# A one-core attention and two-MLP kernel: another conversion of float64 weights, reciprocals spread by transposes, and fewer blocks in plain form

## The chip, the core and the metric

The kernel runs on one core of a Trainium2 chip. A core has TensorE (PE in the profile; its weight loads are PEld), VectorE (DVE), ScalarE (ACT), GpSimd (POOL) and SyncE (SP), which take their instructions in written order, each from its own list, and wait for one another by semaphores; transfers run on DMA queues that SP and POOL feed. The metric is device time in microseconds (us) of one execution, as the median of several runs.

## The reference

The reference is an attention over 4 batches, 12 heads, 448 positions and 64 elements per head, and two MLPs behind it on the 1792 x 768 result:

```
q_n, k_n = rmsnorm(q, g_q), rmsnorm(k, g_k)
scores = q_n @ k_n.T / 8;  scores = scores - max(scores)
attn = exp(scores);  attn = attn / (sum(attn) + 1e-9)
x = (attn @ v), heads side by side             # 1792 x 768
x = (sigmoid(x @ w_gate) * (x @ w_val)) @ w_out    # 768 -> 1536 -> 768
x = relu(x @ w_in) ** 2 @ w_out2                   # 768 -> 2048 -> 768
```

The weights w_gate, w_val, w_out, w_in and w_out2 lie in HBM as float64. Everything else is float32.

## The kernel before, in words

**Sweeps.** The MLPs run batch by batch, in four sweeps (`sweep(s)`, L519) of 448 positions. Each sweep needs all the weights, cut into NB = 68 blocks of 128 x 768 numbers: 24 of w_gate and w_val by turns, 12 of w_out, 16 of w_in, 16 of w_out2. Between the products of sweep s stand the steps of the attention of batch s+1, one slot after another (`slots_of`, L638). Batch 0's attention has no sweep to stand in: it is the prologue (L781), whose steps are laid out by hand as a list of due times, sorted, and kept in that order (`pinned`). Elsewhere the tile scheduler orders each engine's list.

**A product in three passes.** PE multiplies in a fast form of float32 (fp32r) that keeps fewer bits of each factor. So a matrix is split into a high part, its cast to fp32r, and a low part, the remainder, and `mm3` (L510 to 512) adds three products: high by high, high by low, low by high. A block's weights are split by `w_split` (L155): ACT casts the high part (L164), DVE subtracts (L165), both into one of four buffers `wsp`. x is split by `x_hi` (ACT, L334) and `x_lo` (DVE, L337).

**Plain products.** In sweep 0 the first NPLAIN = 12 blocks of w_gate and w_val are multiplied in plain float32 (L539), from batch 0's unsplit x, `xplain`. For these blocks the conversion writes straight into the `wsp` buffer, and `w_split` only stores it.

**The conversion.** In sweep 0 each block goes through four steps, which `w_ahead` (L168) issues some blocks ahead of the product:

- `w_load` (L110, L116): SP issues the load of the float64 block, 768 KB, into one of three buffers `raw`. Seen as pairs of 32-bit words, `lo` and `hi`.
- `w_conv` (L123): ACT scales `hi`, read as a float, by 2^-112 (L137), which moves the exponent to float32's place and leaves three bits of room; DVE takes the sign bit out of `hi` (L140), shifts ACT's result left by three and puts the sign back (L144), and puts in the top three bits of `lo` (L146). The result is a float32 block in `wraw` (three buffers) or, for plain blocks, in `wsp`.
- `w_store` (L153): POOL issues the store of the float32 block to a DRAM copy, `w`, 384 KB.
- `w_split`, as above.

Sweeps 1 to 3 load the float32 copies (L116's other branch, w into wraw), without conversion. The prologue's plan has the loads of blocks 0 to 4 and the conversions of blocks 0 and 1; further ones come where `w_ahead` finds room when block 0's product is issued, which is ahead of the prologue's last steps in the scheduler's view.

**Attention of batches 0 and 1.** A pair of heads `hp` is one unit; there are six pairs a batch. Per pair: a transpose of q and k (`a_mm`, `a_copy`, L256 and its neighbours), scores of four chunks of 112 rows (`s_mm`, L262), their maximum on DVE (L268), exponentials with sums `su` on ACT (L280, two a chunk), transposes of the result p (`c_mm`, L295) and copies of these (`c_copy`, L304 on ACT and a DVE copy), then `pv_mm` (L307): the product with v (L313), and a spread of the reciprocals. For that spread, `s_rec` (L285) takes the reciprocals of `su`, 112 x 4 x 2 numbers (L288), and eight small float32 matmuls against the identity (L318) write each of them into the 64 rows of its head in PSUM, 128 x 448. ACT copies it (`x_rec`, L326) and DVE multiplies (`x_sum`). Batches 2 and 3 divide otherwise, and use none of this.

**Rings.** Three `raw`, three `wraw`, four `wsp`, and four temporaries `tmp` (L54) of 128 x 512 that attention (squares, `rs`) and the MLPs (gate, ReLU, outputs) share. PSUM: four accumulators `acc` and two `att`.

Of the kernel before, what the change touches and what calls it, by code (L numbers as in the profile page):

```python
# [8 lines left out]
F32 = mybir.dt.float32  # L9
F32R = mybir.dt.float32r  # L10
I32 = mybir.dt.int32
AF = mybir.ActivationFunctionType
ALU = mybir.AluOpType
# [4 lines left out]
def attention_moe_moe2_kernel(  # L18
# [14 lines left out]
    nc = tc.nc  # L33
    B, H, S, D = q.shape
# [3 lines left out]
    KD = DM // 128  # L38
    K1 = F1 // 128
    K2 = F2 // 128  # L40
    HP = H // 2
    QC = 4
    QR = S // QC
# [4 lines left out]
    scale = 1.0 / float(D) ** 0.5  # L48
# [5 lines left out]
    tmp_p = ctx.enter_context(tc.tile_pool(name="tmp", bufs=4))  # L54
# [8 lines left out]
    ident = const.tile([128, 128], F32, name="ident")  # L63
# [33 lines left out]
        for kb in range(K2 // 2):  # L97
            one_sweep.append(rows64(w_out2, 2 * kb, 2, hf * 384, 384))
    NB = len(one_sweep)
    NPLAIN = K1  # L100
    NALL = NB * B

    w32 = [dram_p.tile([128, 768], F32, tag=f"w{i}", name=f"w{i}") for i in range(NB)]
# [19 lines left out]
    def w_conv():  # L123
        i = pos["conv"]
        pos["conv"] += 1
        if i >= NB:
            return
        r = raw64.pop(i).rearrange("p (f t) -> p f t", t=2)
        lo, hi = r[:, :, 0], r[:, :, 1]
        if i < NPLAIN:  # L130
            sp = wsp_p.tile([128, 2, 768], F32R, tag="wsp", name="wsp")
            t = sp[:, 0].bitcast(F32)
            wsp[i] = sp
        else:
            t = wraw_p.tile([128, 768], F32, tag="wraw", name="wraw")
        ti = t.bitcast(I32)
        size = nc.scalar.activation(out=t, in_=hi.bitcast(F32), func=AF.Copy, scale=2.0 ** -112)  # L137
        if pinned[0]:
            tc.keep_in_program_order(size)
        sign = nc.vector.tensor_scalar(  # L140
            out=hi, in0=hi, scalar1=-(2 ** 31), scalar2=None, op0=ALU.bitwise_and)
        if pinned[0]:
            tc.keep_in_program_order(sign)
        nc.vector.scalar_tensor_tensor(  # L144
            out=ti, in0=ti, scalar=3, in1=hi, op0=ALU.logical_shift_left, op1=ALU.bitwise_or)
        nc.vector.scalar_tensor_tensor(  # L146
            out=ti, in0=lo, scalar=29, in1=ti, op0=ALU.logical_shift_right, op1=ALU.bitwise_or)
        wraw[i] = t

    def w_store():  # L150
# [4 lines left out]
    def w_split():  # L155
        i = pos["split"]
        pos["split"] += 1
        if pos["store"] <= i < NB:
            w_store()
        t = wraw.pop(i)  # L160
        if i < NPLAIN:
            return
        sp = wsp_p.tile([128, 2, 768], F32R, tag="wsp", name="wsp")
        nc.scalar.copy(out=sp[:, 0], in_=t)  # L164
        nc.vector.tensor_tensor(out=sp[:, 1], in0=t, in1=sp[:, 0].bitcast(F32), op=ALU.subtract)  # L165
        wsp[i] = sp

    def w_ahead(i):  # L168
        while True:
            if pos["split"] <= min(i + 3, pos["conv"] - 1):  # L170
                w_split()
            elif pos["conv"] <= min(i + (3 if pos["conv"] < NPLAIN + 2 else 4), pos["load"] - 1, pos["split"] + 2):
                w_conv()
# [111 lines left out]
    def s_rec(st):  # L285
        su = st["su"]
        nc.vector.tensor_scalar(out=su, in0=su, scalar1=1e-9, scalar2=None, op0=ALU.add)
        nc.vector.reciprocal(out=su, in_=su)  # L288

    def c_mm(st, c, lo, hi):  # L290

# [15 lines left out]
    def pv_mm(st, o, rt):  # L307


        v, pt = st["v"], st.pop("pt")  # L310
        for kc in range(NF + 1):
            for e in range(2):
                nc.tensor.matmul(  # L313
                    out=o[e * D:(e + 1) * D], lhsT=v[:, kc, e], rhs=pt[:, (NF + 1) * e + kc if kc < NF else NF],
                    start=(kc == 0), stop=(kc == NF))
        for c in range(QC):
            for e in range(2):
                nc.tensor.matmul(  # L318
                    out=rt[e * D:(e + 1) * D, c * QR:(c + 1) * QR],
                    lhsT=st["su"][:, c, e:e + 1].to_broadcast([QR, D]), rhs=ident[:QR, :QR],  # L320
                    start=True, stop=True)
        st["o"], st["rt"] = o, rt

    def x_rec(st):
# [9 lines left out]
    def x_hi(st):  # L334
        nc.scalar.copy(out=xtile[st["b"]][:, 0, st["hp"]], in_=st["o"])

    def x_lo(st):  # L337
        x, hp = xtile[st["b"]], st["hp"]
        nc.vector.tensor_tensor(out=x[:, 1, hp], in0=st.pop("o"), in1=x[:, 0, hp].bitcast(F32), op=ALU.subtract)
# [144 lines left out]
    xtile, xplain = {}, {}  # L484
# [34 lines left out]
    def sweep(s):  # L519
# [11 lines left out]
        for m in range(K1):  # L531
            for i in range(2):
                o = acc_tile()[:, :N]
                wb = block()
                for kk in range(KD):
                    if s == 0 and m == 0 and i == 0 and kk == KD - 1:
                        yield
                    if s == 0 and 2 * m + i < NPLAIN:
                        nc.tensor.matmul(  # L539
                            out=o, lhsT=wb[:, 0, kk].bitcast(F32), rhs=xplain[0][:, kk],  # L540
                            start=(kk == 0), stop=(kk == KD - 1))
                    else:
                        mm3(o, wb, kk, x[:, 0, kk], x[:, 1, kk], kk == 0, kk == KD - 1)
                if s == 0 and 2 <= 2 * m + i < 2 + KD:
                    st = {"b": 0, "hp": 2 * m + i - 2, "o": xplain[0][:, 2 * m + i - 2]}
                    x_hi(st)
                    x_lo(st)
                if i == 0:
                    t = tmp("t")
                    e = tmp("e")  # L550
                    nc.scalar.activation(out=e, in_=o, func=AF.Relu, scale=-1.0)
                    nc.scalar.activation(out=t, in_=o, func=AF.Abs)
                    nc.scalar.activation(out=e, in_=e, func=AF.Exp, scale=-1.0)
                    nc.scalar.activation(out=t, in_=t, func=AF.Tanh, scale=0.5)
                else:
                    nc.vector.tensor_tensor(out=e, in0=o, in1=e, op=ALU.mult)
                    nc.vector.scalar_tensor_tensor(out=e, in0=t, scalar=1.0, in1=e, op0=ALU.add, op1=ALU.mult)
                    nc.scalar.copy(out=ht[:, 0, m], in_=e)
                    low.tensor_tensor(out=ht[:, 1, m], in0=e, in1=ht[:, 0, m].bitcast(F32), op=ALU.subtract)
                yield  # L560
        y = xbuf(s)
        for j2 in range(KD // 2):
            for i in range(2):
                o = acc_tile()[:, :N]
                for b2 in range(2):
# [4 lines left out]
                    if b2 == 1:  # L570
# [3 lines left out]
                            out=y[:, 1, j], in0=o, scalar=0.5, in1=y[:, 0, j].bitcast(F32),  # L574
                            op0=ALU.mult, op1=ALU.subtract)
# [7 lines left out]
        for m2 in range(K2 // 2):  # L583
            for i in range(2):
                m = 2 * m2 + i
                o = acc_tile()[:, :N]
# [3 lines left out]
                t = tmp("rl")  # L590
# [5 lines left out]
                for dst, d0, c0, cn in parts:  # L596
                    low.tensor_tensor(
                        out=dst[:, 1, m, d0:d0 + cn], in0=r2[:, c0:c0 + cn],
                        in1=dst[:, 0, m, d0:d0 + cn].bitcast(F32), op=ALU.subtract)
# [5 lines left out]
        for hf in range(2):  # L605
            accs = [acc_tile() for _ in range(nt)]
            for kb in range(K2 // 2):
                wb = block()
                for c, (rr, c0, row) in enumerate(chunks):
                    o = accs[c][:, :384]  # L610
# [283 lines left out]
    for r in range(2):  # L894
# [3 lines left out]
        out=gqk, in0=gains[:, 0:1], scalar=scale, in1=gains[:, 1:2], op0=ALU.mult, op1=ALU.mult)  # L898
# [49 lines left out]
```

## Time and profile before

| | |
|---|---|
| time, median of 3 runs | 1309.39 us (1307.68 to 1309.93) |
| the profiled execution | 1309.2 us, its span 1307.1 us |
| PE | 1284.9 us busy, 98% of the span, mean granted clock 0.997 |
| DVE | 938.4 us, 72% |
| ACT | 781.7 us, 60% |
| POOL | 130.3 us, 10% |
| DMA | 189.62 MB |

The span is the time from the first instruction to the last; the execution's own time has 2.1 us around it. The engines run side by side, so that shares do not add up. A share is an average over parts that differ: the prologue (to about 98 us), sweep 0 with its conversions (to about 430 us), and the three sweeps behind it.

### The profile page before, as it was taken

To read this page: it belongs to the slowest core of one execution; us is meant where nothing else is said; L and a number is where in the kernel's file an instruction comes from. 1 tells how busy PE (TensorE), PEld (TensorE's weight loads), DVE (VectorE), ACT (ScalarE), POOL (GpSimd) and SP (SyncE) were. 2 spreads that over 40 slices of the span, in tenths; PEclk is the share of its full clock that TensorE was granted. 3 is DMA by queue.
4 is the path that set the end of the run, shared out by engine and by line. 5 is a ranking of instruction groups with operands and counts; after the bars stand their busy time and mean duration, and the time that the engine had idled before them with its cause. 6 is when DMAs were issued, how large, how long until landed. Compare 5 with 4: busy or idle time off the path is not lost.

```text
span 1307.1 us, 19338 instructions
## 1 busy us (share of the span) xinstructions
PE 1284.9 (98%) x6899; PEld 1120.1 (86%) x6899; DVE 938.4 (72%) x1643; ACT 781.7 (60%) x1600; POOL 130.3 (10%) x100
## 2 busy tenths in 40 slices
PE   8999999999899999999999999999999999999998
PEld 6554488788697999999999999999999999999998
DVE  6876999899898678768986478877897544435521
ACT  5764687568666678656664477765676455524421
POOL 3201214210221001000010000100010000000000
PEclk9999999999899999999999999999999999999999
DMA  5426897787788434333343533434324343333331
GB/s 144 103 76 216 273 292 246 252 270 218 245 232 273 130 113 121 105 114 107 107 113 105 146 97 110 125 100 114 99 86 121 116 127 109 109 109 109 108 114 46
DMA packets 155807, 189.62 MB, mean 145 GB/s; under 512 B 76096, under 2 KB 119616, under 8 KB 155712
## 3 DMA queue, kind: packets, MB, share of 16 engines
q1 hardware_dynamic: 148416, 161.19, 43.0%
q0 software_dynamic: 5440, 26.74, 5.0%
q8 instruction: 55, 0.90, 0.3%
q10 hardware_dynamic: 1856, 0.46, 0.2%
q14 instruction: 40, 0.33, 0.1%
HBM read 150.60 MB, written 32.24 MB: 140 GB/s over the span
## 4 chain that ended last, share of the span: by engine, by line
PE 73%; issue 10%; DVE 7%; DMA 4%; ACT 4%; POOL 2%; POOLq 0%; ACTq 0%; SPq 0%; DVEq 0%
PE acc L510 15%; PE acc L511 15%; PE acc L512 15%; PE acc L617 5%; PE acc L615 5%; PE acc L616 5%; PE att L398 3%; PE att L439 2%; DMA w<-wraw 2%; PE att L470 2%; POOL ms L232 1%; DVE nm L268 1%; PE att L472 1%; ACT p L280 1%; PE acc L313 1%
## 5 line engine op out<-in xcount | busy, mean ns | idle before, releaser
L165 DVE TENSOR_TENSOR wsp<-wraw,wsp 128x768 fp32r<-128x768 f32 x260 | 248.0, 954 | 130.8 <-ACT wsp L164 125.9
L510 PE MATMUL acc<-xy,wsp 128*128 128x448 f32 x888 | 326.7, 368 | 0.2 <-ACT rl L592 0.2
L512 PE MATMUL acc<-xy,wsp 128*128 128x448 f32 x888 | 326.1, 368 | 0.0
L511 PE MATMUL acc<-xy,wsp 128*128 128x448 f32 x888 | 325.9, 367 | 0.0
L164 ACT CAST wsp<-wraw 128x768 fp32r<-128x768 f32 x260 | 216.6, 834 | 130.9 <-PE acc L617 64.7
L512 PEld LDWEIGHTS acc<-xy,wsp 128*128 128x128 f32 x888 | 166.9, 188 | 16.1 <-issue 2.7
L510 PEld LDWEIGHTS acc<-xy,wsp 128*128 128x128 f32 x888 | 166.8, 188 | 16.1 <-issue 0.9
L511 PEld LDWEIGHTS acc<-xy,wsp 128*128 128x128 f32 x888 | 166.9, 188 | 15.0 <-issue 1.5
L232 POOL TENSOR_TENSOR ms<-ms,mhalf 112x16 f32<-112x16 f32 (+1 forms) x25 | 91.1, 3648 | 577.1 <-DVE ms L231 486.8
L616 PE MATMUL acc<-wsp,rb 128*128 128x384 f32 x384 | 129.2, 336 | 0.0
L617 PE MATMUL acc<-wsp,rb 128*128 128x384 f32 x384 | 129.0, 336 | 0.0
L615 PE MATMUL acc<-wsp,rb 128*128 128x384 f32 x384 | 128.8, 335 | 0.0
L510 PE MATMUL acc<-hb,wsp 128*128 128x448 f32 x288 | 106.2, 369 | 0.0
L511 PE MATMUL acc<-hb,wsp 128*128 128x448 f32 x288 | 105.5, 367 | 0.0
L512 PE MATMUL acc<-hb,wsp 128*128 128x448 f32 x288 | 105.5, 367 | 0.0
L417 ACT ACTIVATE p<-att,nm,ms 112x448 f32<-112x448 f32 x96 | 68.8, 724 | 34.7 <-DVE nm L408 34.5
L137 ACT ACTIVATE wraw<-raw 128x768 f32<-128x768 f32 x56 | 51.5, 920 | 51.8 <-DMA w<-wraw 27.8
L592 ACT ACTIVATE rl<-acc 128x448 f32<-128x448 f32 x64 | 35.0, 547 | 70.7 <-PE acc L512 69.9
L280 ACT ACTIVATE p<-att,nm 112x448 f32<-112x448 f32 x88 | 55.3, 639 | 33.7 <-DVE nm L268 32.3
L617 PEld LDWEIGHTS acc<-wsp,rb 128*128 128x128 f32 x384 | 72.1, 188 | 1.6 <-issue 1.3
L616 PEld LDWEIGHTS acc<-wsp,rb 128*128 128x128 f32 x384 | 72.1, 188 | 0.8 <-issue 0.7
L615 PEld LDWEIGHTS acc<-wsp,rb 128*128 128x128 f32 x384 | 72.1, 188 | 0.2
(136 smaller groups left out, 2167.7 us busy)
## 6 DMA issues: line engine op xcount, KB each, us to landing
wraw<-w SPq DMA_DIRECT2D x204, 384.0 KB, 3.0
w<-wraw POOLq DMA_DIRECT2D x56, 384.0 KB, 6.0
raw<-in_moe_w_out_dram SPq DMA_DIRECT2D x28, 768.0 KB, 5.4
raw<-in_moe_w_in_dram SPq DMA_DIRECT2D x16, 768.0 KB, 6.6
raw<-in_moe_w_gate_dram SPq DMA_DIRECT2D x12, 768.0 KB, 6.8
raw<-in_moe_w_val_dram SPq DMA_DIRECT2D x12, 768.0 KB, 6.1
out_dram<-ob SPq DMA_DIRECT2D x28, 192.0 KB, 2.9
qs<-qs SPq DMA_DIRECT2D x24, 224.0 KB, 3.0
```

Of the source, the lines that this page charges most:

```text
L137: size = nc.scalar.activation(out=t, in_=hi.bitcast(F32), func=AF.Copy, scale=2.0 ** -112)
L164: nc.scalar.copy(out=sp[:, 0], in_=t)
L165: nc.vector.tensor_tensor(out=sp[:, 1], in0=t, in1=sp[:, 0].bitcast(F32), op=ALU.subtract)
L232: nc.gpsimd.tensor_tensor(out=ms, in0=ms, in1=mhalf[:QR, 0:ms.shape[1]], op=ALU.pow)
L280: nc.scalar.activation(out=p[:, e], in_=ps[:QR, e, :S], func=AF.Exp, bias=nm[:, e:e + 1], scale=st["rq"][:, c, e:e + 1] if "rq" in st else ...
L417: nc.scalar.activation(out=p[:, i * (S + TAIL):i * (S + TAIL) + S], in_=ps[:QR, i, :S], func=AF.Exp, bias=nm[:, i:i + 1], scale=rq[:, 2 * ...
L510: nc.tensor.matmul(out=o, lhsT=wh, rhs=xh, start=start, stop=False)
L511: nc.tensor.matmul(out=o, lhsT=wh, rhs=xl, start=False, stop=False)
L512: nc.tensor.matmul(out=o, lhsT=wl, rhs=xh, start=False, stop=stop)
L615: nc.tensor.matmul(out=o, lhsT=rh, rhs=wh, start=(k1 == 0), stop=False)
L616: nc.tensor.matmul(out=o, lhsT=rh, rhs=wl, start=False, stop=False)
L617: nc.tensor.matmul(out=o, lhsT=rl, rhs=wh, start=False, stop=(k1 == K2 - 1))
```

## The change

1. **NPLAIN** goes from 12 to 4: blocks 4 to 11 of sweep 0 are converted into `wraw`, split and multiplied in three passes.
2. **The conversion** has one DVE step less. ACT's function becomes a leaky one (`Prelu`, scale 2^-112, alpha 2^32): a negative number comes out 2^32 times larger, by which a bit stands where the shift by three leaves it as the sign. DVE's first step shifts `lo` right by 29 (into `hi`), its second shifts ACT's result and puts these three bits in. The third step goes.
3. **Reciprocals**: `s_rec` also lets POOL write `su` 64 times over into a temporary `sb` of 112 x 512, and `pv_mm` takes four transposes of it instead of eight matmuls. This holds for the twelve pairs of batches 0 and 1.
4. **x's split** for batch 0 moves from blocks 2 to 7 (one pair each) to blocks 0 to 2 (two pairs each), since block 4 needs it now.

```
-    NPLAIN = K1
+    NPLAIN = 4
...
-        size = nc.scalar.activation(out=t, in_=hi.bitcast(F32), func=AF.Copy, scale=2.0 ** -112)
+        size = nc.scalar.activation(
+            out=t, in_=hi.bitcast(F32), func=AF.Prelu, scale=2.0 ** -112, alpha=2.0 ** 32)
...
-        sign = nc.vector.tensor_scalar(
-            out=hi, in0=hi, scalar1=-(2 ** 31), scalar2=None, op0=ALU.bitwise_and)
+        low3 = nc.vector.tensor_scalar(
+            out=hi, in0=lo, scalar1=29, scalar2=None, op0=ALU.logical_shift_right)
...
         nc.vector.scalar_tensor_tensor(
             out=ti, in0=ti, scalar=3, in1=hi, op0=ALU.logical_shift_left, op1=ALU.bitwise_or)
-        nc.vector.scalar_tensor_tensor(
-            out=ti, in0=lo, scalar=29, in1=ti, op0=ALU.logical_shift_right, op1=ALU.bitwise_or)
...
         nc.vector.reciprocal(out=su, in_=su)
+        sb = st["sb"] = tmp_p.tile([128, 512], F32, tag="tmp", name="sb")[:QR].rearrange(
+            "p (c e d) -> p c e d", c=QC, e=2)
+        nc.gpsimd.tensor_copy(out=sb, in_=su.unsqueeze(3).to_broadcast([QR, QC, 2, D]))
...
+        sb = st.pop("sb")
         for c in range(QC):
-            for e in range(2):
-                nc.tensor.matmul(
-                    out=rt[e * D:(e + 1) * D, c * QR:(c + 1) * QR],
-                    lhsT=st["su"][:, c, e:e + 1].to_broadcast([QR, D]), rhs=ident[:QR, :QR],
-                    start=True, stop=True)
+            nc.tensor.transpose(
+                rt[:, c * QR:(c + 1) * QR], sb[:, c].rearrange("p e d -> p (e d)"), ident[:QR, :QR])
...
-                if s == 0 and 2 <= 2 * m + i < 2 + KD:
-                    st = {"b": 0, "hp": 2 * m + i - 2, "o": xplain[0][:, 2 * m + i - 2]}
-                    x_hi(st)
-                    x_lo(st)
+                if s == 0 and 2 * m + i < KD // 2:
+                    for hp in range(2 * (2 * m + i), 2 * (2 * m + i) + 2):
+                        st = {"b": 0, "hp": hp, "o": xplain[0][:, hp]}
+                        x_hi(st)
+                        x_lo(st)
```

The change also moves instructions on the engines' lists. From about 430 us on, all five lists stand as before. At the prologue's end, ACT's list holds the conversions of the blocks ahead (L137, told apart by the number of their `raw` buffer), the exponentials of the last two pairs (L280, after the change L279) and the copies of their transposes (L304, after the change L306). This is the stretch around the fifth pair's last chunks, before:

```order
L137 ACTIVATE wsp<-raw_598 128x768
L256 ACTIVATE kq<-acc,gqk 128x448
L280 ACTIVATE p,su<-att,nm 112x448 x2
L326 COPY rs<-acc 128x448
L304 COPY pt<-acc 128x4x112
L335 CAST xy_232<-xplain 128x448
L280 ACTIVATE p,su<-att,nm 112x448 x2
L304 COPY pt<-acc 128x4x112
L280 ACTIVATE p,su<-att,nm 112x448 x2
```

and after the change:

```order
L137 ACTIVATE wsp<-raw_596 128x768
L255 ACTIVATE kq<-acc,gqk 128x448
L279 ACTIVATE p,su<-att,nm 112x448 x2
L326 COPY rs<-acc 128x448
L306 COPY pt<-acc 128x4x112
L335 CAST xy_232<-xplain 128x448
L137 ACTIVATE wraw<-raw_915 128x768
L279 ACTIVATE p,su<-att,nm 112x448 x2
L306 COPY pt<-acc 128x4x112 x2
L279 ACTIVATE p,su<-att,nm 112x448 x2
```

Here raw_598 and raw_596 are block 1, raw_915 is block 4: its conversion now stands ahead of two exponentials. A little further on the same list, at the last pair, before:

```order
L280 ACTIVATE p,su<-att,nm 112x448 x4
L326 COPY rs<-acc 128x448
L304 COPY area<-acc 128x4x112
L335 CAST xy_232<-xplain 128x448
L280 ACTIVATE p,su<-att,nm 112x448 x2
L137 ACTIVATE wsp<-raw_710 128x768
L137 ACTIVATE wsp<-raw_826 128x768
L304 COPY area<-acc 128x4x112 x2
```

and after:

```order
L137 ACTIVATE wraw<-raw_1067 128x768
L279 ACTIVATE p,su<-att,nm 112x448 x2
L326 COPY rs<-acc 128x448
L306 COPY area<-acc 128x4x112
L279 ACTIVATE p,su<-att,nm 112x448 x2
L137 ACTIVATE wsp<-raw_706 128x768
L137 ACTIVATE wsp<-raw_819 128x768
L335 CAST xy_232<-xplain 128x448
L137 ACTIVATE wraw<-raw_1069 128x768
L306 COPY area<-acc 128x4x112 x2
```

Blocks 2 and 3 (raw_710 and raw_826, now raw_706 and raw_819) keep their place; the conversions of blocks 5 and 6 (raw_1067 and raw_1069) are new here, block 6's ahead of the last two copies. On POOL, which issues the stores (w with a number is a block's DRAM copy, 97 that of block 0), the same stretch reads before:

```order
L232 TENSOR_TENSOR ms<-ms,mhalf 112x16 x5
L153 DMA w_97<-wsp 128x768
L153 DMA w_98<-wsp 128x768
L153 DMA w_99<-wsp 128x768
L153 DMA w_100<-wsp 128x768
L232 TENSOR_TENSOR ms<-ms,mhalf 112x16
L153 DMA w_101<-wsp 128x768
```

and after:

```order
L231 TENSOR_TENSOR ms<-ms,mhalf 112x16
L152 DMA w_97<-wsp 128x768
L290 COPY sb<-su 112x512
L152 DMA w_98<-wsp 128x768
L152 DMA w_101<-wraw 128x768
L290 COPY sb<-su 112x512
L152 DMA w_102<-wraw 128x768
L290 COPY sb<-su 112x512
L152 DMA w_99<-wsp 128x768
L152 DMA w_100<-wsp 128x768
L152 DMA w_103<-wraw 128x768
```

The stores of blocks 4 and 5 (w_101, w_102) now stand ahead of those of blocks 2 and 3, and the copies of `su` between them.

## Rows read from the trace of the kernel before

**Rows 1.** Windows: length, busy PE, PEld, DVE, ACT, POOL; PE clock, DMA share, GB/s.

```profile
98.00:430.00 332.00, 320.37 (x1640) 248.04 (x1639) 290.54 (x429) 218.55 (x428) 68.39 (x71) 0.99 0.80 251
430.00:1307.00 877.00, 873.83 (x4668) 817.92 (x4667) 576.92 (x1087) 500.11 (x1018) 40.96 (x11) 1.00 0.37 109
```

**Rows 2.** Waits of PE from 98 us on: tile, releaser, us, times, longest.

```profile
PE att L313 <- ACT pt L304: 3.4, 1, 3.4
```

**Rows 3.** Timeline of PE: start, us, line; plain and three-pass products.

```profile
119.54 3.55 PE L539 MATMUL acc<-xplain,wsp 128*128 128x448 f32 x9
...
123.31 8.45 PE L539 MATMUL acc<-xplain,wsp 128*128 128x448 f32 x22
...
249.84 0.37 PE L512 MATMUL acc<-hb,wsp 128*128 128x448 f32 x1
...
252.88 0.37 PE L512 MATMUL acc<-hb,wsp 128*128 128x448 f32 x1
```

**Rows 4.** Timeline of PE in the prologue, the third pair's last product.

```profile
81.53 3.23 PE L313 MATMUL acc<-pt,v 128*64 128x448 f32 x16
84.59 0.94 PE L318 MATMUL acc<-ident,su 112*64 112x112 f32 x16
85.46 0.89 PE L295 MATMUL acc<-ident,p 112*128 112x112 f32 x7
86.28 1.01 PE L262 MATMUL att<-kq 64*112 64x448 f32 x4
```

**Rows 5.** Lines of DVE, 98 to 430 us: busy, mean ns | idle before, releasers.

```profile
L165 DVE TENSOR_TENSOR wsp<-wraw,wsp 128x768 fp32r<-128x768 f32 x58 | 55.1, 954 | 4.2 <-ACT wsp L164 3.5 <-DMA wraw<-w 0.6
...
L146 DVE SCALAR_TENSOR_TENSOR wraw<-raw,wraw 128x768 int32<-128x768 int32 x56 | 53.3, 952 | 0.2
...
L140 DVE TENSOR_SCALAR raw<-raw 128x768 int32<-128x768 int32 x64 | 35.8, 559 | 13.9 <-ACT wraw L137 10.4 <-ACT wsp L137 3.1
```

**Rows 6.** Lines of ACT, 98 to 430 us, columns as above.

```profile
L137 ACT ACTIVATE wraw<-raw 128x768 f32<-128x768 f32 x56 | 51.5, 920 | 51.8 <-DMA w<-wraw 27.8 <-DVE wsp L165 15.0 <-issue 2.5
...
L280 ACT ACTIVATE p<-att,nm 112x448 f32<-112x448 f32 x48 | 30.1, 635 | 23.8 <-DVE nm L268 23.8
```

**Rows 7.** Timeline of ACT and PE near 340 us, with idle; one window.

```profile
337.48 0.89 ACT L137 ACTIVATE wraw<-raw 128x768 f32<-128x768 f32 x1 [3.57 <-DMA w<-wraw]
...
341.60 6.19 PE L313 MATMUL att<-pt,v 128*64 128x448 f32 x16 [3.38 <-ACT pt L304]
...
340.00:348.00 8.00, 6.40 (x26) 4.28 (x28) 7.11 (x9) 3.64 (x6) 1.08 (x2) 0.57 0.63 178
```

**Rows 8.** Timeline of ACT, DVE and SP's queue in the prologue.

```profile
69.33 0.92 ACT L137 ACTIVATE wsp<-raw 128x768 f32<-128x768 f32 x1
...
76.91 0.63 ACT L280 ACTIVATE p<-att,nm 112x448 f32<-112x448 f32 x1 [1.75 <-DVE nm L268]
...
71.88 0.96 DVE L146 SCALAR_TENSOR_TENSOR wsp<-raw,wsp 128x768 int32<-128x768 int32 x1
...
73.39 0.54 SPq L116 DMA_DIRECT2D raw<-in_moe_w_gate_dram  x1
```

**Rows 9.** Timeline of one raw load and its reader; the queue's list.

```profile
112.92 0.37 SPq L116 DMA_DIRECT2D raw<-in_moe_w_val_dram  x1
...
118.08 0.91 ACT L137 ACTIVATE wsp<-raw 128x768 f32<-128x768 f32 x1 [4.30 <-DMA raw<-in_moe_w_val_dram]
...
raw<-in_moe_w_gate_dram SPq DMA_DIRECT2D x12, 768.0 KB, 6.8
```

**Rows 10.** Timeline of POOL: one operation early and one late.

```profile
222.16 7.65 POOL L232 TENSOR_TENSOR ms<-ms,mhalf 112x16 f32<-112x16 f32 x1 [0.72 <-DVE ms L231]
...
548.55 2.90 POOL L232 TENSOR_TENSOR ms<-ms,mhalf 112x16 f32<-112x16 f32 x1 [40.63 <-DVE ms L231]
```

**Rows 11.** Source views of two lines: ns min/median/max, first and last start.

```profile
L288 DVE RECIPROCAL su<-su x12: 191/196/203, 27.2 to 413.7; 112x8 f32<-112x8 f32 x12
...
L318 PE MATMUL att<-ident,su x96: 257/259/262, 193.7 to 425.3; 112*64 112x112 f32 x96
```

More of the change, by code (lines that the diff above doesn't have):

```diff
@@ L136, in w_conv @@
         ti = t.bitcast(I32)
-        size = nc.scalar.activation(out=t, in_=hi.bitcast(F32), func=AF.Copy, scale=2.0 ** -112)
+        size = nc.scalar.activation(
+            out=t, in_=hi.bitcast(F32), func=AF.Prelu, scale=2.0 ** -112, alpha=2.0 ** 32)
         if pinned[0]:
             tc.keep_in_program_order(size)
-        sign = nc.vector.tensor_scalar(
-            out=hi, in0=hi, scalar1=-(2 ** 31), scalar2=None, op0=ALU.bitwise_and)
+        low3 = nc.vector.tensor_scalar(
+            out=hi, in0=lo, scalar1=29, scalar2=None, op0=ALU.logical_shift_right)
         if pinned[0]:
-            tc.keep_in_program_order(sign)
+            tc.keep_in_program_order(low3)
         nc.vector.scalar_tensor_tensor(
             out=ti, in0=ti, scalar=3, in1=hi, op0=ALU.logical_shift_left, op1=ALU.bitwise_or)
-        nc.vector.scalar_tensor_tensor(
-            out=ti, in0=lo, scalar=29, in1=ti, op0=ALU.logical_shift_right, op1=ALU.bitwise_or)
         wraw[i] = t
```

## The prediction

> **What bounds the kernel now.** I read the views in this order: windows, waits, lines, then the timeline of a few places. The two windows [rows 1] split the span where the program splits it. From 430 us on PE is busy 873.83 of 877 us, and in the written order of all five engines nothing differs there, so nothing can be gained or lost in that part. What can move is the first 430 us: the prologue (batch 0's attention, to about 98 us) and sweep 0, in which every weight block is converted, stored and split. In 98 to 430 us PE is busy 320.37 of 332 us, DVE 290.54 (88%) and ACT 218.55. PE still sets the pace, with 11.6 us in which it stands idle. Its largest wait, 3.4 us, ends at ACT's copies [rows 2], but ACT was itself late: in front of the steps that PE lacked at 338 us it stood 3.57 us at the head of its queue on a conversion whose buffer was not free, because the store out of it (w<-wraw) had not landed [rows 7]. Over the sweep ACT lost 27.8 us to such stores and 15.0 us to DVE's split [rows 6]. A store is issued after DVE's last conversion step, so both waits begin with a late DVE. I read DVE as the second bound of sweep 0, after PE's own work.
>
> **Eight blocks off the plain form.** A plain product takes two records; 22 of them last 8.45 us and 9 last 3.55 us [rows 3], so that one more takes (8.45-3.55)/13 = 0.377 us and a product 0.753 us. In the three-pass form two like matmuls stand 249.84 and 252.88 us apart over five triples [rows 3]: 0.608 us a product. 8 blocks x 6 products x 0.145 us = **7.0 us less on PE**. It costs ACT 8 casts and DVE 8 splits of 0.954 us [rows 5], 7.6 us, which lie beside PE's 18 passes of 0.203 us, 3.65 us a block. If that cover were gone it would cost the 7.6 us.
>
> **Reciprocals by transposes.** The 16 records of the old form fill 84.59 to 85.46 us, 0.87 us a pair; seven transposes behind them fill 85.46 to 86.28 us [rows 4], so four take 0.47 us. Gain 0.40 us for each of 12 pairs: **2.4 us in sweep 0**, 2.4 us in the prologue (counted there).
>
> **The conversion on DVE.** The third step goes away: in the sweep 64 of them, as many as L140 has, by 0.952 us, 60.9 us [rows 5], and four more in the prologue. The new first step is a one-source integer operation of the old one's shape (L140, 0.559 us [rows 5]), and I cost it the same. ACT's step changes its function; no row has that function. Bounds: as now, 0.92 us [rows 6], or twice that. I take 0.92, as shape and operands are the same. The Trainium skill, "ScalarE: Activation LUTs", section "Step-by-step: what each stage is for", says that an element takes one cycle whatever the function; no run here shows it yet for this one. So DVE falls from 290.5 to about 290.5-60.9+7.6 = 237 us of 332.
>
> **What that is worth to PE.** The 11.6 us idle, and behind the longest gap PE ran at half clock: a 16-record product that takes 3.23 us at 81.53 [rows 4] took 6.19 us at 341.60 [rows 7], and the window shows a mean granted clock of 0.57 of 2.4 GHz, so some of it at 1.2 GHz. Together 11.6+3.0 = 14.6 us. Bounds: none of it comes back (the store's landing stays as slow, and three buffers hold it up as before) or all. The split and store start one step of 0.95 us and its queue earlier in every block, but the landing itself does not change, so I take two thirds: **9.5 us**.
>
> **The prologue is where the change costs.** Blocks 4 to 6 are now converted into the ring of three, so their conversions no longer wait for a plain buffer, and the written order puts two of them between the exponentials of batch 0's last two pairs and a third before the last copies. Each load needs the raw buffer that the conversion before it frees, a chain: conversion, load, conversion, load. In the trace of before, block 1's ACT step starts at 69.33 us, and DVE's third step at 71.88 us; the load that follows is issued at 73.39 [rows 8], 0.55 us after that step's end. Without the step it issues at about 72.4 us. A load takes 118.08-112.92 = 5.1 us by the one that ACT can be seen to wait for, and 6.8 us by the queue's median [rows 9]. So block 4 lands at 77.5 to 79.2 us. ACT was free from 75.16 us (76.91 less its idle 1.75 us [rows 8]) and now stands at the head of its queue for that load; behind it are the exponentials that began at 76.91. They begin, with the 0.92 us of the conversion, at 78.4 to 80.1 us: 1.5 to 3.2 us late, and PE's transposes wait for them. Block 5's wait is longer (its load can start only after two DVE steps and a maximum), but PE has block 0's first products to run there, and I cost it at 0 to 2.5 us. Block 6: from the end of block 5's step, DVE needs 1.6 us, the issue 0.55, the load 5.1 to 6.8 and the step 0.92, 8.2 to 9.9 us, and only then come the two copies that the last pair's product needs; ACT's own steps in between, four exponentials of 0.635 us, two conversions [rows 6] and three copies of some 0.5 us, are an estimated 6 us, and part of what is left lies beside waits that are there now. I cost it at 1 to 3 us. Sum 2.5 to 8.7 us; I take 6.9, above the middle, since other loads and stores run by then; less 2.4 us of transposes in six pairs, about **4.5 us lost, net** with the bounds 0 and 7, and 3 us more if one of these gaps halves the clock as the one of 3.38 us did.
>
> **The copy on POOL.** No row has such a copy. Bounds: nothing, or as slow as the slowest operation on POOL, 7.65 us [rows 10]. In sweep 0 it is hidden: the last reciprocal is at 413.7 us and the records that used it end at 425.3 us [rows 11]. I take nothing; for the last pair of the prologue, which PE needs at once, the upper bound could show as some 5 us. One operation on POOL takes 2.90 us at 548 us, where DVE is less busy, and 7.65 us in sweep 0 [rows 10]. The Trainium skill, "SBUF — State Buffer", section "Who interferes with whom", says that GpSimd and VectorE operations with two SBUF inputs or two ports exclude each other for a whole instruction. The stretched row agrees; by that rule each of 12 copies could also hold a DVE step back for as long as it lasts, which the 95 us that DVE then has to spare would cover.
>
> **Moved x splits.** They need the prologue's last product, as before, and their ACT and DVE steps were already issued in the prologue; nothing.
>
> **Sum.** The profiled execution took 1309.2 us (span 1307.1), 0.2 us under the median 1309.39. 1309.2-7.0-2.4-9.5+4.5 = 1294.8; put on the median, **1295 us**.
>
> **Rivals.** *The prologue loses nothing* (0.20): loads land in 5 us or less and PE has other work; then 4.5 us come off, and the transposes' 2.4 us too: 1288. For it: loads of the prologue run beside few other transfers. *The waits of sweep 0 stay* (0.18): stores, not DVE, hold the three buffers, or the new function on ACT costs double (64 x 0.92 = 59 us more), which makes ACT what DVE was. Then only PE's own work is saved: 1309.4-9.4+4.5 = 1304.5, and 1307 to 1310 with the prologue at its upper end; the conversion would then not do what it says. For it: the 27.8 us on landings [rows 6]. *Slower* (0.12): the spread reciprocal holds one of four temporaries from POOL's copy to PE's transposes, 11 us for the last pair by rows 11. ACT's gate, square and ReLU steps need the same four. If one of them stands at the head of ACT's queue as long as the conversion at 337.48 did, PE pays 3.4 us of idle and 3.0 us of half clock [rows 7], 6.4 us. Against 14.4 us of net gain that decides from three of the six pairs on: 1295+19.2 = 1314. Against it: no ACT wait of before ends at a temporary, and DVE, which frees most of them, gets faster.
>
> **How the numbers follow.** Forecast 0.50, its own range 1289 to 1301; the others as above. 1284 to 1307 leaves out the slower case, the upper end of the second rival, and little below. What a measurement can tell from no change is 0.2%, 2.6 us. Faster: all of the first two and two thirds of the third, 0.82; same 0.08 (the rest of the third, a little of the last); slower 0.10.
>
> **What would show it.** Right: in the windows, DVE near 237 of some 315 us in sweep 0 and PE's idle there 3 to 5 us; two or three waits of ACT's conversion on raw loads between 74 and 100 us, of 2 to 5 us, with PE idle behind them; the last prologue product ending near 102 instead of 97.6 us; block 4 in three passes at once behind block 3. Wrong: ACT's step over 1 us; ACT waits on stores still near 28 us; PE waiting for the transposed reciprocals; a granted clock under 1 in several windows.

## The result and the profile after

The changed kernel takes 1292.4 us (median of 4 runs, 1289.3 to 1297.4), against 1308.5 us before: a ratio of 0.988, 95% interval 0.9845 to 0.9916, so 16.1 us less. The forecast was 1295. The profiled execution is the longest of the four, 1297.4 us with a span of 1295.6; a second profile of the same kernel, below, has a span of 1291.6.

The windows of the changed kernel, cut where the prologue's last product ends and where the part begins that is alike in both (columns as in [rows 1]; span 1295.6 us):

```profile
0.00:102.60 102.60, 93.82 (x522) 52.52 (x522) 71.14 (x129) 65.78 (x158) 26.75 (x27) 0.93 0.53 139
102.60:418.50 315.90, 310.01 (x1616) 255.15 (x1616) 244.53 (x367) 224.32 (x433) 63.06 (x74) 0.99 0.79 252
418.50:1295.00 876.50, 873.84 (x4668) 817.99 (x4667) 576.70 (x1087) 499.77 (x1018) 41.01 (x11) 1.00 0.38 109
```

The last row answers to the second of [rows 1]: PE is busy there for 873.84 us against 873.83, with as many records, so nothing was won or lost in that part. In the sweep PE's idle time fell from 11.6 to 5.9 us (315.90 less 310.01), while DVE's load fell from 290.5 to 244.5 us. The prologue runs at a mean granted clock of 0.93.

The waits of ACT's conversion in 98 to 418 us of the changed kernel (us in total, times, longest), and the lines of the conversion and of POOL's copy:

```profile
ACT wraw L137 <- DVE wsp L164: 17.7, 17, 1.8
...
ACT wraw L137 <- DMA w<-wraw: 4.5, 2, 3.1
```

```profile
L137 ACT ACTIVATE wraw<-raw x64: 883/911/985, 77.3 to 404.0; 128x768 f32<-128x768 f32 x64
...
L290 POOL COPY sb<-su x12: 604/612/983, 29.6 to 394.1; 112x512 f32<-112x512 f32 x12
```

The wait for stores, 27.8 us in [rows 6], is down to 4.5 (7.2 in the second profile). The wait for DVE's split, 15.0 us there, is not smaller, 17.7 us; PE's idle time fell all the same. The leaky function takes 0.911 us for a block, as the scaling did, and a copy on POOL takes 0.612 us, near the lower of the two bounds.

The end of the prologue, ACT's and PE's timeline of the changed kernel (start, us, line, idle before and its releaser):

```profile
77.29 0.89 ACT L137 ACTIVATE wraw<-raw 128x768 f32<-128x768 f32 x1 [3.91 <-DMA raw<-in_moe_w_gate_dram]
78.08 0.63 ACT L279 ACTIVATE p<-att,nm 112x448 f32<-112x448 f32 x1
...
86.30 0.92 ACT L137 ACTIVATE wraw<-raw 128x768 f32<-128x768 f32 x1 [1.76 <-DMA raw<-in_moe_w_val_dram]
...
96.01 0.89 ACT L137 ACTIVATE wraw<-raw 128x768 f32<-128x768 f32 x1 [1.84 <-DMA raw<-in_moe_w_gate_dram]
```

```profile
78.85 1.22 PE L297 MATMUL acc<-ident,p 112*128 112x112 f32 x7 [3.77 <-ACT p L279]
...
97.37 0.51 PE L297 MATMUL acc<-ident,p 112*128 112x112 f32 x3 [1.78 <-ACT area L306]
...
99.42 3.22 PE L315 MATMUL acc<-area,v 128*64 128x448 f32 x14
```

The three conversions stand there for their loads as forecast, for 3.91, 1.76 and 1.84 us (the forecast said 2 to 5 us each); behind the first, PE is idle for 3.77 us because the exponentials come late, behind the third for 1.78 us because the copies do. The last product of the prologue ends at 99.42 + 3.22 = 102.6 us; before, PE was done with it at 97.6 us.

### The profile page after: what moved, and what is told of

Its sections match the earlier page's. It is cut to its first block, busy times and chain, and to the rows that moved or that the text cites. A ratio compares the mean times of both kernels' runs of the same rounds, so it can differ in the third digit from the quotient of the medians.

```text
span 1295.6 us, 19119 instructions
## 1 busy us (share of the span) xinstructions
PE 1277.7 (99%) x6803; PEld 1125.7 (87%) x6803; DVE 892.4 (69%) x1583; ACT 789.9 (61%) x1608; POOL 130.8 (10%) x112
## 4 chain that ended last, share of the span: by engine, by line
PE 89%; DVE 3%; DMA 2%; ACT 2%; issue 2%; SPq 1%; POOL 1%; ACTq 0%; DVEq 0%; POOLq 0%
PE acc L510 18%; PE acc L512 18%; PE acc L511 18%; PE acc L616 6%; PE acc L618 6%; PE acc L617 6%; PE att L398 3%; PE att L439 2%; PE att L261 2%; PE att L470 2%; PE att L315 1%; PE att L472 1%; PE att L243 1%; PE acc L539 1%; ACT p L279 1%
## 5 line engine op out<-in xcount | busy, mean ns | idle before, releaser
L164 DVE TENSOR_TENSOR wsp<-wraw,wsp 128x768 fp32r<-128x768 f32 x268 | 256.4, 957 | 143.5 <-ACT wsp L163 134.7
L510 PE MATMUL acc<-xy,wsp 128*128 128x448 f32 x936 | 345.0, 369 | 0.4 <-ACT rl L593 0.4
L512 PE MATMUL acc<-xy,wsp 128*128 128x448 f32 x936 | 344.5, 368 | 0.0
L511 PE MATMUL acc<-xy,wsp 128*128 128x448 f32 x936 | 343.8, 368 | 0.0
L163 ACT CAST wsp<-wraw 128x768 fp32r<-128x768 f32 x268 | 223.6, 834 | 140.8 <-PE acc L618 77.4
L512 PEld LDWEIGHTS acc<-xy,wsp 128*128 128x128 f32 x936 | 176.3, 188 | 17.5 <-issue 3.3
L510 PEld LDWEIGHTS acc<-xy,wsp 128*128 128x128 f32 x936 | 176.2, 188 | 16.9 <-issue 1.3
L511 PEld LDWEIGHTS acc<-xy,wsp 128*128 128x128 f32 x936 | 176.2, 188 | 16.3 <-issue 1.5
L231 POOL TENSOR_TENSOR ms<-ms,mhalf 112x16 f32<-112x16 f32 (+1 forms) x25 | 84.8, 3397 | 569.8 <-DVE ms L230 479.4
L137 ACT ACTIVATE wraw<-raw 128x768 f32<-128x768 f32 x64 | 58.4, 914 | 40.5 <-DVE wsp L164 17.7
L279 ACT ACTIVATE p<-att,nm 112x448 f32<-112x448 f32 x88 | 55.2, 635 | 17.5 <-DVE nm L267 15.1
```

What stands on the lines that cost most here:

```text
L231: nc.gpsimd.tensor_tensor(out=ms, in0=ms, in1=mhalf[:QR, 0:ms.shape[1]], op=ALU.pow)
L279: nc.scalar.activation(out=p[:, e], in_=ps[:QR, e, :S], func=AF.Exp, bias=nm[:, e:e + 1], scale=st["rq"][:, c, e:e + 1] if "rq" in st else ...
L510: nc.tensor.matmul(out=o, lhsT=wh, rhs=xh, start=start, stop=False)
L511: nc.tensor.matmul(out=o, lhsT=wh, rhs=xl, start=False, stop=False)
L512: nc.tensor.matmul(out=o, lhsT=wl, rhs=xh, start=False, stop=stop)
```

## The experiments

All times are medians of 4 to 12 runs; the ratios are to runs of the kernel before on the same chip, whose medians were 1306.5 to 1308.9 us. "Prologue" is the end of its last product in the profiled execution; in all of these kernels ten records of block 0 are done by then. "Sweep 0" goes from there to the first of PE's last 4,694 records; both columns are of one execution. From that record to the end the profiles take 881.8 to 882.7 us, but for the one with 4 plain blocks alone, 880.3 us: there twelve more records of the MLP stand ahead of batch 1's last product, so that the same count begins some 1.5 us later and its sweep reads that much too long.

| kernel | us (range) | ratio to before, 95% interval | prologue, us | sweep 0, us |
|---|---|---|---|---|
| before | 1308.5 (1307.2 to 1309.9) | | 97.6 | 327.7 |
| changed | 1292.4 (1289.3 to 1297.4) | 0.9845 to 0.9916 | 102.6 | 311.2 |
| conversion alone | 1296.0 (1294.3 to 1297.9) | 0.9883 to 0.9915 | 98.4 | 314.7 |
| transposes alone | 1307.6 (1305.5 to 1311.4) | 0.998 to 0.9998 | 93.3 | 331.0 |
| 4 plain blocks alone | 1310.6 (1308.1 to 1313.7) | 1.0001 to 1.002 | 103.5 | 322.5 |
| changed, no transposes | 1297.4 (1295.8 to 1298.9) | 0.9898 to 0.9925 | 107.2 | 307.6 |
| changed, 12 plain blocks | 1293.0 (1291.9 to 1294.3) | 0.9866 to 0.9897 | 94.8 | 315.9 |
| changed, old conversion | 1307.2 (1302.6 to 1310.6) | 0.9977 to 1.0003 | 98.7 | 325.0 |
| changed, loaded DVE | 1302.7 (1296.7 to 1309.2) | 0.9941 to 0.9974 | 98.3 | 318.2 |
| changed, conversions held | 1289.3 (1288.5 to 1290.5) | 0.9839 to 0.9868 | 94.6 | 311.7 |
| changed, NPLAIN = 6 | 1287.4 (1286.8 to 1288.2) | 0.9834 to 0.9867 | 92.6 | 311.2 |
| changed, NPLAIN = 8 | 1286.7 (1285.7 to 1289.9) | 0.9833 to 0.9871 | 92.6 | 309.4 |
| the same, matmuls in batch 1 | 1287.1 (1285.8 to 1288.9) | 0.9808 to 0.9853 | 94.5 | 309.9 |
| changed, again | 1292.2 (1290.8 to 1293.6) | 0.9873 to 0.9904 | 102.4 | 307.4 |

**The conversion alone.** The kernel before with the change's ACT and DVE steps of `w_conv` and nothing else.

> The kernel before with the leaky conversion alone; 12 blocks stay plain, reciprocals stay matmuls. The prediction's theory (a late DVE is behind the stores' waits): 1297 to 1302 us, DVE near 230 us busy in the sweep's 332, ACT's conversion waiting well under 28 us for stores, and the prologue ends at 97 to 98 us as before. Rival (the stores' landing holds the three buffers, whatever DVE does): 1307 to 1310 us with the stores' row near 28 us.

It took 1296.0 us, a little under the span expected, so the theory holds and the rival falls. The sweep's window of this kernel:

```profile
98.40:413.10 314.70, 311.70 (x1613) 241.53 (x1613) 240.99 (x364) 218.65 (x426) 58.39 (x71) 1.00 0.82 261
```

PE is idle for 3.0 us of 314.7 at full clock, as many records as before took 327.7 us. Of the 14.6 us of idle time and half clock that the prediction counted, 13.0 came back, not 9.5. DVE is busy for 241.0 us, where 230 was expected. No wait for a store is left among ACT's conversions there. They wait for DVE's split instead, of which PE's idle time shows little:

```profile
ACT wraw L137 <- DVE wsp L164: 25.3, 27, 2.2
```

The stores come earlier by more than the removed step. Taken over blocks 12 to 67 of both traces, the median time from the end of ACT's step (L137) to POOL's issue of the store was 5.31 us before and is 2.16 us here, 3.15 us less for a removed step of 0.952 us. From issue to landing a store takes a median of 6.00 us before and 6.25 us here.

**The old conversion in the changed kernel**, the counterpart: the four lines of the old `w_conv` put back.

> The changed kernel with the old conversion of three DVE steps. Theory (DVE is the sweep's second bound): the conversion is most of the gain, 1303 to 1309 us, DVE near 300 us busy in the sweep, ACT's conversions waiting 20 us or more for stores and splits, PE idle 10 us or more in the sweep. Rival (with fewer plain blocks the step is covered by PE's longer blocks): 1293 to 1298 us.

1307.2 us, 14.8 us more: nearly all of the change's gain. Its waits in 98 to 418 us:

```profile
ACT wraw L137 <- DMA w<-wraw: 44.8, 23, 4.0
ACT wsp L164 <- DVE wraw L146: 8.9, 7, 1.7
```

Stores held ACT for 44.8 us, more than the 27.8 of before; eight more blocks go through the three buffers here (with 4 plain blocks alone, below, the wait is 32.6 us).

**DVE loaded, the chain left short.** An added step reads the block just converted and writes six numbers that nobody needs:

```
+        nc.vector.tensor_reduce(
+            out=scr, in_=t.rearrange("p (a b) -> p a b", b=128), axis=AX.X, op=ALU.max)
         wraw[i] = t
```

> The changed kernel with one added DVE step for each converted block, a maximum over the block just converted that nothing reads, some 0.8 us; it leaves out nothing. It loads DVE as the removed step did, but the store does not wait for it. Theory 1 (DVE's load is what counts, since its list is in order and all else waits in it): 1300 to 1306 us. Theory 2 (the length of the chain from load to store counts, by which three buffers are held): 1292 to 1295 us.

The step takes 0.944 us, like the removed one. The sweep's window and ACT's first wait:

```profile
98.30:416.40 318.10, 308.95 (x1588) 252.52 (x1589) 290.16 (x430) 223.18 (x431) 64.34 (x74) 0.98 0.79 249
```

```profile
ACT wraw L138 <- DMA w<-wraw: 19.7, 11, 3.7
```

DVE is back at 290 us, and the time at 1302.7: 10.3 of the 14.8 us come with DVE's load by itself, though no store waits for the added step itself. The stores are late all the same: from the end of ACT's step to the issue of the store the median is 4.87 us, against 2.40 in the changed kernel and 6.75 with the old conversion. The other 4.5 us, to the old conversion's 1307.2, are left for the store that waits for one step more; that is a subtraction, not a run. Both theories had a part, the first the larger; the runs of this kernel spread over 12.5 us, so that the shares are rough.

**Transposes alone.** The kernel before with `sb` and the four transposes.

> The kernel before with the transposed reciprocals alone. The prediction's theory: 0.40 us for each of 12 pairs, 1304 to 1307 us. Rival 1 (PE waited for something else at these places, so its saving is idle time): 1308 to 1310 us. Rival 2 (the spread reciprocal holds one of four temporaries and ACT waits for it): 1311 us or more, with waits of ACT on the transposes that read sb.

1307.6 us, 1.3 less (0.3 to 2.6 by the interval): under the saving as costed, just outside rival 1's span, and not rival 2. The two parts went opposite ways: the prologue 4.3 us shorter, the sweep 3.3 us longer. In the prologue the scheduler also wrote another order: `pinned` keeps the order of the conversions and of a few other steps there, and the exponentials and PE's products are left to the scheduler. PE's timeline of this kernel behind the second pair's product, and below it that of before:

```profile
45.02 0.60 PE L321 MATMUL acc<-ident,sb 112*128 112x112 f32 x4
45.55 1.01 PE L262 MATMUL att<-kq 64*112 64x448 f32 x4
46.49 0.89 PE L298 MATMUL acc<-ident,p 112*128 112x112 f32 x7
```

```profile
46.12 0.94 PE L318 MATMUL acc<-ident,su 112*64 112x112 f32 x16
46.99 0.89 PE L295 MATMUL acc<-ident,p 112*128 112x112 f32 x7
47.81 1.76 PE L262 MATMUL att<-kq 64*112 64x448 f32 x8
49.50 0.89 PE L295 MATMUL acc<-ident,p 112*128 112x112 f32 x7
51.43 1.22 PE L295 MATMUL acc<-ident,p 112*128 112x112 f32 x7 [1.04 <-ACT p L280]
```

Before, the next pair's scores (L262) came behind a block of transposes, their maxima and exponentials were late, and PE stood for 1.04 us, in three of the pairs. Now four of the eight score matmuls come first and the wait is gone. PE is busy for 88.6 us of the prologue against 90.4 before, so that of the 4.3 us 1.7 are less work and 2.6 less idle time. In the sweep of this profile PE runs at half clock for 20.5 us, against 7 before. Two of its rows:

```profile
156.00:166.00 10.00, 8.50 (x34) 7.31 (x35) 9.54 (x16) 6.62 (x15) 2.74 (x4) 0.66 0.91 289
394.00:412.00 18.00, 12.33 (x52) 11.52 (x52) 9.29 (x14) 8.90 (x21) 3.00 (x4) 0.62 0.72 241
```

**The changed kernel without transposes.** The eight matmuls back, no `sb`.

> The changed kernel with the eight matmuls back in place of POOL's copy and the transposes. The prediction's theory: 2.4 to 4.8 us above the changed kernel's 1292.4, 1295 to 1297 us. Rival 1 (the transposes save nothing): 1292 to 1293 us. Rival 2 (the copy and its temporary cost time): 1288 to 1291 us.

1297.4 us, 5.0 more than the changed kernel's 1292.4, as the theory's upper end. By the ratios to the kernel before, the two sets of runs of the changed kernel lie 4.1 and 3.0 us below it, and the intervals overlap a little, so that the size is rough. The prologue ends 4.6 us later (17.1 us of it at half clock, against 13.7 in the changed kernel's, which may be part of this); the sweep is no longer than the changed kernel's, 307.6 against 311.2 and 307.4. So the six pairs in the sweep saved nothing that shows. One place differs: PE's list takes the transposes of batch 2's first q and k (L243) where the exponentials are not done. The row of the changed kernel, then the one without transposes:

```profile
393.45 1.18 PE L243 MATMUL att<-ident,qk 112*128 112x112 f32 x8 [2.44 <-ACT p L279]
```

```profile
399.68 0.93 PE L243 MATMUL att<-ident,qk 112*128 112x112 f32 x8
```

**Plain blocks alone.** The kernel before with NPLAIN = 4 and the moved x splits.

> The kernel before with 4 plain blocks instead of 12 and the moved x splits alone. The prediction's theory: 7.0 us less PE work, and as much lost in the prologue where conversions stand in front of exponentials; with 7.6 us more on a DVE that is already late 1306 to 1312 us, the prologue ending at 102 to 106 us. Rival (the prologue's loss has another cause than these conversions, the transposes for one): 1300 to 1304 us, the prologue ending at 97 to 99 us.

1310.6 us, 1.7 more (0.1 to 2.6 by the interval), so no gain. In the profile, an execution of 1308.7 us, the prologue ends 5.9 us later and the sweep is 6.7 us shorter, its extra 1.5 us taken off. The rival falls; the conversions cost the prologue without any transposes.

**Twelve plain blocks in the changed kernel.** NPLAIN and the x splits as before.

> The changed kernel with 12 plain blocks again and x split at blocks 2 to 7: leaky conversion and transposes alone. Theory (fewer plain blocks save 7.0 us of PE's work and lose as much in the prologue): 1290 to 1294 us, equal to the changed kernel's 1292.4, the prologue ending at 93 to 95 us and the sweep 7 us longer than the changed kernel's. Rival (the 7.0 us are kept and nothing is lost): 1298 us or more. If conversion and transposes only add (12.9 and 1.3 us): 1294.7 us.

1293.0 us, with the prologue at 94.8 us and a sweep of 315.9: no difference that these runs can tell, made of two that nearly cancel.

**Conversions held.** The exponentials and `rs` copies of the last two pairs and the conversions of blocks 4 to 6 are kept in the order in which they are written:

```
-        if pinned[0]:
+        if pinned[0] or NPLAIN <= i < NPLAIN + 3:
             tc.keep_in_program_order(size)
```

(and the same call behind each of the others, for `st["hp"] > 3`).

> The changed kernel, with the conversions of blocks 4 to 6 kept behind the prologue's last exponentials and copies in ACT's list; nothing else differs. Theory (these conversions, standing for their raw loads, cost the prologue some 7 us, half clock behind the 3.8 us gap included): 1284 to 1288 us, the last prologue product ending at 93 to 97 us instead of 102.6. Rival (blocks 4 to 6 then come late and PE waits for them instead): 1290 to 1293 us, with PE waiting for the splits or ACT's casts between 110 and 130 us.

The prologue ends 8.0 us earlier, at 94.6, and the median falls by 3.1 us only, to 1289.3. Both had a part: the sweep is 4.3 us longer than in the second profile of the changed kernel (311.7 against 307.4). Blocks 4 to 6 then come late, and PE waits for their splits, as the waits of 94 to 130 us show:

```profile
PE acc L516 <- DVE wsp L164: 1.7, 3, 0.7
PE att L243 <- ACT kq L251: 1.1, 1, 1.1
PE acc L514 <- ACT wsp L163: 0.4, 1, 0.4
```

**NPLAIN = 6, NPLAIN = 8, and the change again** (one number in the diff), on one chip.

> The changed kernel with NPLAIN = 6. Blocks 4 and 5 are then converted into the ring of four, whose buffers are not free before the first blocks are multiplied, so that no conversion of a block beyond 3 stands among the prologue's last exponentials. Theory (the prologue's loss hangs on that ring alone; a block off the plain form saves 0.87 us): the prologue ends at 94 to 96 us, 1286 to 1289 us in all. Rival (the place of the conversions is set by the blocks ahead, not by the ring, or the loss comes back in the sweep): 1291 to 1294 us.

> The changed kernel with NPLAIN = 8. Theory: the prologue as with 6, and 2 x 0.87 = 1.7 us more work of PE, 1288 to 1291 us. Rival (the same as the changed kernel's): 1292 us or more.

> The changed kernel once more, unaltered, so that its time stands beside the two others of the same chip. Theory: 1291 to 1295 us, and the half-clock stretch that its profile showed at 18 to 29 us is not there in every execution, since the same list ran there at full clock in the kernel before.

In both the prologue ends at 92.6 us, 9.8 us before the changed kernel's 102.4; 8.0 of that are the held conversions of the run above, and about 2 a half-clock stretch at its start (last section). In both of ACT's lists the conversions of blocks 2 and 3 are the only ones among the last exponentials and copies, so the ring into which blocks 4 and 5 are converted decides it. With 8 the sweep has neither half clock nor late blocks. PE's timeline with NPLAIN = 8, the last pair, and with 6, block 4:

```profile
86.09 1.68 PE L297 MATMUL acc<-ident,p 112*128 112x112 f32 x14
87.93 0.97 PE L315 MATMUL acc<-area,v 128*64 128x448 f32 x2 [0.16 <-ACT area L306]
```

```profile
110.24 2.58 PE L539 MATMUL acc<-xplain,wsp 128*128 128x448 f32 x3 [3.15 <-DVE wsp L145]
```

With 6 the conversions of blocks 6 and 7 stand ahead of 4's, and PE waits 3.15 us for block 4, which takes the 1.7 us of saved work back. Both are 5 us faster than the change (1287.4 and 1286.7 against 1292.2 on the same chip), and cannot be told apart: their ranges overlap. So the expectation that 8 costs 1.7 us more than 6 did not come true, as it had left out the late blocks.

**NPLAIN = 8 with matmuls in batch 1.**

> The kernel with NPLAIN = 8, with transposed reciprocals in the prologue's six pairs alone; the six pairs of batch 1 spread them by the eight matmuls again. Theory (in the sweep the transposes bring nothing, since with them PE's list takes the transposes of batch 2's first q and k earlier, where they wait for ACT's exponentials): 1285 to 1287.5 us, equal to NPLAIN = 8, with no wait of PE over 0.5 us at those transposes near 383 us. Rival (the sweep's six pairs save 2.4 us): 1288 to 1290 us.

1287.1 us, the sweep 309.9 us against 309.4, and no wait at L243 in the sweep. With the transposes, PE's work in the sweep is less by nearly what was costed, 306.1 us busy against 308.1, but it stands idle for 1.4 us more, 3.3 against 1.9, of which 1.08 us ahead of L243. So the transposes' place is the prologue; in the sweep they neither gain nor cost time.

## Why the prediction was right, step by step

The main mechanism, a late DVE that delays the stores, and the price in the prologue are borne out. That the sum came within 3 us of the result is in part luck, since the sizes of its terms were off both ways and nearly cancel.

- **Eight blocks off the plain form, 7.0 us.** Conversion alone to conversion with four plain blocks: 314.7 to 307.6 us in the sweep, 7.1.
- **The conversion, 9.5 us.** The mechanism was right and the size low: 13.0 us. "Two thirds", because "the landing itself does not change", underrated it: the landing did not change (6.00 and 6.25 us), but the waits for stores all but went. With a DVE that is on time each store starts earlier than the one step saved, 3.15 us for 0.952, since DVE's list is in order and everything in it came late. That the wait for DVE's split begins with a late DVE too is not borne out: it was 15.0 us before, 25.3 with the conversion alone and 17.7 after. DVE's own figure, 237 us, was low against 244.5, although three of the 64 blocks are now converted ahead of the sweep. Steps that stand back to back overlap (in the changed kernel one that begins at 147.09 takes 0.55 us, and the next begins at 147.56), and there is less of this where DVE has room: summed over the sweep it is 30.6 us before and 19.9 after. So a removed row of 0.952 us gives back less than that.
- **Transposes, 2.4 us in the sweep and 2.4 in the prologue.** This step failed in both places: no time came off the sweep, and 4.3 to 4.6 us came off the prologue. The cost per pair was near, 0.34 us by the starts of the two rows behind the second pair's product against 0.40; what the lists do with it was not foreseen. That the total, 3.0 to 5.0 us by the runs without transposes, is near the 4.8 is luck.
- **The prologue's waits, 6.9 us.** From held to changed 8.0 us. The places and causes were as worked out; part of the excess is half clock behind the 3.77 us (a mean of 0.66 in 79 to 84 us, last section), which the prediction named as 3 us more and left out of the sum.
- **Nothing for POOL's copy.** 0.612 us, hidden, and PE never waited for the transposed reciprocals. The Trainium skill, "SBUF — State Buffer", section "Who interferes with whom", has a VectorE operation with two inputs in SBUF and a GpSimd operation that reads SBUF hold each other up. The trace agrees: the longest copy, 0.983 us, begins at 210.74 us beside such a subtraction of DVE (L164, 0.96 us from 210.29), and of the 268 subtractions the longest, 1.66 us against a median of 0.957, begins at 257.61 us with a copy beside it (0.62 us from 257.82). A product (L560) at 162.28 us took 1.08 us beside a third copy instead of 0.62, and a step with one input (L141) at 92.93 us 0.82 us beside a fourth instead of 0.56. The second profile shows the same places. Beside a DVE step that reads PSUM no copy was longer than 0.613 us.
- **Nothing for the moved x splits.** They were not run by themselves; four plain blocks alone holds them, and its sweep shows 6.7 of the 7.0 us.
- **ACT's function.** 0.911 us against 0.920 with the old one. The Trainium skill, "ScalarE: Activation LUTs", section "Step-by-step: what each stage is for", has an element take one cycle whatever the function; the trace agrees.
- **The rivals.** That the prologue loses nothing was wrong: 8.0 us. That the sweep's waits stay was wrong: 27.8 to 4.5 us. No wait of ACT for a temporary appeared, so the slower case had no ground. What could have made the change slower was another thing, the prologue's waits for raw loads without the conversion's gain, as 1310.6 us with the plain blocks alone show.
- **The signs.** DVE's load and PE's idle time came near what was said, and the end of the prologue and block 4 as said. One sign of being wrong came too, a granted clock under 1 in several windows: four stretches, 20.5 us in all, in the first profile of the changed kernel, and three, 17.1 us, in the second. The prediction had one such stretch as a possible 3 us; the last section has rows of some of them.

The measured steps of sweep and prologue, -13.0 - 7.1 + 8.0 - 4.3 = -16.4, give 1292.1 from 1308.5. They are picked from single profiles of different kernels, and the half clock at the prologue's start is not among them. Against the forecast's terms the conversion gave 3.5 us more and the prologue's transposes 1.9 more, while the sweep's transposes gave 2.4 less and the prologue's waits took 1.1 more. That the parts alone add to 12.5 us only (12.9 + 1.3 - 1.7) and the whole is 16.1 was not traced to one cause; the 20.5 us at half clock in the profile of transposes alone may be part of it.

## What to carry to other kernels

Where an engine's list is in order and nearly full, a step costs not only what waits for it but everything that stands behind it: an added step that nothing waits for cost 10.3 us here. Look for whose waits end at that engine, one stage on. A buffer ring that is not free also keeps work out of a stretch: moving blocks to a freer ring let their conversions slip in front of steps that the last product needed, and six or eight plain blocks, which these runs cannot tell apart, were better than four or twelve. After a change, read the lists again in places that the diff does not touch: here the scheduler wrote PE's list otherwise in both the prologue and the sweep, for reasons that were not tried, and that decided what the transposes were worth.

## What the runs showed of the hardware

In the two profiles of the changed kernel, PE's gaps of 2.2 to 3.9 us were followed by stretches of some 3.4 us at half clock (1.2 GHz), its gaps of 1.6 and 1.8 us were not. The length of one gap does not decide it: in the kernel before a gap of 2.04 us, ended at 164.23 us, was not followed by one, and in the kernel with the loaded DVE gaps of 0.97 and 0.96 us, ended at 391.43 and 393.28 us, were, from 394.2 us on. So the same list lost more in one execution than in the other: near 393 us PE waited 2.44 us and ran at half clock behind it in the first, 1.56 us and at full clock in the second. Rows of the first and the second profile (us, busy times, granted clock, DMA share, GB/s):

```profile
18.00:28.00 10.00, 9.88 (x37) 5.34 (x36) 5.74 (x12) 5.67 (x15) 2.90 (x1) 0.53 0.56 126
79.00:84.00 5.00, 4.89 (x20) 2.45 (x19) 4.25 (x8) 3.82 (x12) 1.15 (x2) 0.66 0.30 66
...
393.00:399.00 6.00, 5.55 (x29) 5.55 (x30) 2.00 (x5) 5.25 (x13) 1.15 (x2) 0.72 0.68 217
```

```profile
391.00:396.00 5.00, 4.95 (x35) 4.96 (x36) 1.41 (x4) 4.85 (x11) 0.93 (x2) 1.00 0.76 245
```

Not expected was the half clock at 18 to 28 us, where PE had no gap over 0.6 us. The second profile of the changed kernel has it too, against the expectation that it comes and goes, but others do without it. It was there in 6 of the 14 profiles, those whose full clock began at 4.2 to 5.0 us, and in none of the seven where it began at 5.9 to 7.4 us; one that began at 5.0 went without. What sets that beginning was not tried, nor whether it is the cause. The kernel with NPLAIN = 8 and the one with matmuls in batch 1 have the same prologue, but end it at 92.6 and 94.5 us, the second with that stretch: it costs about 2 us.
